# Attention, routed experts and a rational FFN in one launch: the last group's token ids placed ahead of its gates

## Chip, cores and metric

One core of a Trainium2 chip runs the whole program. The metric is the device time of one launch in microseconds (us); of several launches the median counts.

## What is computed

The reference chains three layers in fp32. Weights and activations are random normals.

```python
def _attn_ref(q, k, v):                      # 2 batches, 8 heads, 768 steps, 64 wide
    for t in range(S):
        state = gamma * state + outer(k[t], v[t])
        y[t] = scale * (q[t] @ state)

def _moe_ref(x, w_gate, w1, w2, capacity):   # 1536 tokens, 512 wide, 8 experts, 384 slots
    expert_idx = argmax(x @ w_gate); gate_w = softmax(...)[expert_idx]
    # token i takes the next slot of its expert, in the order of the tokens
    y = relu(disp @ w1) @ w2
    out[i] = gate_w[i] * y[expert_idx[i], pos[i]]

def _moe2_ref(x, w_in, w_out, a, b):
    h = x @ w_in
    g = (a0 + a1*h + a2*h**2 + a3*h**3) / (1 + |b0|*|h| + |b1|*h**2 + 1e-6)
    return g @ w_out
```

## The kernel before, in words

The order of the work on each engine is written out by hand (a manual schedule): every engine, and every DMA queue, does its own instructions strictly in the order of the code.

**Attention** (`attention`, L571) walks 12 units of 128 tokens; units 0 to 5 are one batch and 6 to 11 the other. For unit u TensorE does `scores` (L286: products of k and q into PSUM), `inter` (L314: the running state against q), `intra` (L332: masked scores against v) and `state` (L300). VectorE masks the scores (`mask`, L294) and scales the result (`attn_xt`, L343); ScalarE copies the state out (L312). `gate_mm` (L352) turns the unit's tokens round and forms the gate logits; `gate_out` (L411) copies the tokens out and SP writes them to the DRAM tensor `xd` (L420). Scores of unit u+1 are formed ahead of `inter(u)` if u is over 1 and behind `state(u)` if u is 0 or 1 (L631, L647). They all use one pair of PSUM banks, tag "s"; `inter` uses the pair "y" from unit 1 on.

**Routing.** The tokens are routed in two groups, units 0 to 6 and 7 to 11. Of a group, `gate_parts` (L383) finds expert and gate, `rank_mm` (L422) counts positions on TensorE, `rank_pos` (L458) turns them into slots, `rank_put` (L482) builds `pe` (a 0/1 matrix of rows) and `rr` (32 columns with the token ids and 32 with the gates, each in the column of its expert's tile), and `place_mm` (L495) multiplies them in full fp32, so that `tab` holds token id and gate of every slot. `rank_mm` of the second group also computes `self.pad` (L435 to L439), how far expert 0's first tile fell short of 128 tokens.

The first group's table gives 128 tokens of expert 0, fetched early (`early_gather`, L680) and put through that expert's first layer in `attn_tail` (L697). There the order on TensorE is: transposes of the fetched tokens (`early_x`), `gate_mm` of unit 11, ten first-layer matmuls (`win_l1`, L731; 12 for each half of the hidden units), `rank_mm`, two more, twelve more, `win_turn` of the first half (four transposes, L750), `place_mm` of the second group (L721), `win_turn` of the second half. VectorE meanwhile splits weights into a high and a low part (`split_lo`, L145; the low part alone is its work) and forms the low part of the turned activations (`win_parts`, L758). `indices` (L520) turns the ids of `tab` into `gidx`.

**Experts.** Then GpSimd (the POOL queue) gathers tiles 1, 2, 3 and on from `xd` (`gather`, L858; `fetch`, L848), which needs `gidx` and all writes to `xd`. `first_expert` (L807) does 14 of expert 0's 24 second-layer matmuls (`win_l2`, L765), turns gathered tile 1 (`expert_x`, L891: four transposes, a copy on ScalarE, a subtraction on VectorE), does the other ten and goes on with tile 1's 96 rows. Experts 1 to 7 and the FFN follow.

**Weight loads.** `load_next` (L160) issues on SP's queue; a load needs one of six `raw` buffers, and a buffer comes free when `split_lo` has read it. `attn_tail` asks for four (L707).

Of the kernel before, what the change touches and what calls it, by code (L numbers as in the profile page):

```python
# [7 lines left out]
F32 = mybir.dt.float32  # L8
# [13 lines left out]
E = 8  # L22
# [58 lines left out]
class Build:  # L81
# [70 lines left out]
    def load_w(self, i, half):  # L152
        nc = self.nc
        raw = self.wp.tile([128, 1024], F32, tag="raw", name="raw", bufs=6)
        sl = slice(half * 1024, half * 1024 + 1024)
        src = self.a["wm"][i] if i < 32 else self.wd[i - 32]
        nc.sync.dma_start(out=raw, in_=src[:, sl])
        self.raw[i, half] = raw

    def load_next(self, n):  # L160
        for _ in range(min(n, self.load_cap - self.nload)):
            self.load_w(self.nload // 2, self.nload % 2)
            self.nload += 1

    def prep_next(self):
# [119 lines left out]

    def scores(self, u):  # L286
        kt, qt = self.feats(u)
        sc = self.sc[u] = self.pair_bank("s", "sc").rearrange("p (r j t) -> p r j t", r=2, j=4)
# [133 lines left out]
    def rank_mm(self, b):  # L422
        nc = self.nc
        u0, u1 = self.units(b)
        g = u1 - u0
        oh = self.oh[:, u0:u1]
        bank = self.bank("rk")
        rk = bank[:, 0 : g * E].rearrange("p (g e) -> p g e", e=E)
        mms = [(rk, self.tri, oh[:, :, 0:E])]
        mms += [(rk[:, d:], self.ones, oh[:, 0 : g - d, 0:E]) for d in range(1, g)]  # L430
        if b:
            mms += [(rk[:, i], self.ones, self.run[:, 0:E]) for i in range(g)]
        for i, (out, w, x) in enumerate(mms):
            nc.tensor.matmul(out, lhsT=w, rhs=x, start=(i == 0), stop=(i == len(mms) - 1))
        if u0 == UA:  # L435
            cnt = bank[:, 64:65]
            nc.tensor.matmul(cnt, lhsT=self.ones, rhs=self.run[:, 0:1], start=True, stop=True)
            nc.vector.tensor_scalar(out=self.pad, in0=cnt, scalar1=-1.0, scalar2=128.0, op0=ALU.mult, op1=ALU.add)
            nc.vector.tensor_scalar(out=self.pad, in0=self.pad, scalar1=0.0, scalar2=None, op0=ALU.max)  # L439
        if u1 == NU:  # L440
            self.cnt = bank[:, 128 : 128 + 2 * E]
            for i in range(g + 1):
                x = oh[:, i - 1] if i else self.run
                nc.tensor.matmul(self.cnt, lhsT=self.ones, rhs=x, start=(i == 0), stop=(i == g))
        else:
# [36 lines left out]
    def rank_put(self, b):  # L482
# [2 lines left out]
        g = u1 - u0  # L485
        n = E * (self.nsub + 1)
        c2, pm, idk, gk = self.where.pop(b)
        at, rr, pe = sm("at", [g, n], bufs=1), sm("rr", [g, 2 * n]), sm("pe", [g, 128])
        tt(out=at, in0=self.over(self.col("slot"), g), in1=self.across(c2, g, n), op=ALU.is_equal)
        tt(out=rr[:, :, 0:n], in0=at, in1=self.across(idk, g, n), op=ALU.mult)  # L490
        tt(out=rr[:, :, n:], in0=at, in1=self.across(gk, g, n), op=ALU.mult)
        tt(out=pe, in0=self.over(self.col("iota"), g), in1=self.across(pm, g, 128), op=ALU.is_equal)
        self.place[b] = (pe, rr)

    def place_mm(self, b, tp=None):  # L495
        nc = self.nc
        pe, rr = self.place.pop(b)
        u0, u1 = self.units(b)
        n = E * (self.nsub + 1)
        tp = (self.bank("tpa", "tp") if tp is None else tp)[:, 0 : 2 * n]  # L500
        for i in range(u1 - u0):
            nc.tensor.matmul(tp, lhsT=pe[:, i], rhs=rr[:, i], start=(i == 0), stop=(i == u1 - u0 - 1))
        tp = tp.rearrange("p (a n) -> p a n", a=2)
        if b == 0:
            nc.vector.tensor_copy(self.tab, tp)
        else:
            nc.vector.tensor_tensor(out=self.tab, in0=self.tab, in1=tp, op=ALU.add)

    def count(self):
        self.nc.vector.tensor_copy(self.off, self.cnt)  # L510
# [60 lines left out]
    def attention(self):  # L571
        nc, tc, a = self.nc, self.tc, self.a
        with ExitStack() as st:
# [45 lines left out]
            for u in range(NU):  # L619
# [8 lines left out]
                    self.y_table(u + 3, pool)  # L628
                for n in LO_AT.get(u, ()):
                    self.split_lo(n // 2, n % 2)  # L630
                if 1 < u < NU - 1:  # L631
                    self.scores(u + 1)
                    self.mask(u + 1)
                if u - 2 in done:
                    next(gate)
                self.inter(u)
                if u - 4 in done:
                    self.place_mm(done[u - 4])
                if u == UA + 3:
                    self.early_gather()  # L640
                self.intra(u)
                if u:
                    self.attn_xt(u)
                if u - 2 in done:
                    next(gate)
                self.state(u)
                if u < 2:  # L647
                    self.scores(u + 1)
                    self.mask(u + 1)
                if u == 0:  # L650
# [22 lines left out]
                    self.rank_pos(done[u - 2])  # L673
                if u - 3 in done and not last:
                    self.rank_put(done[u - 3])
                for n in LO_END.get(u, ()):
                    self.split_lo(n // 2, n % 2)
            self.attn_tail()
# [18 lines left out]
    def attn_tail(self):  # L697
# [6 lines left out]
        self.gate_group(b)  # L704
        self.gate_out(u)
        ps.append(self.pair_bank("y", "l1")[:, 0:512])
        self.load_next(4)  # L707
        self.rank_mm(b)
        self.rank_pos(b)
        self.h0 = self.wp.tile([128, 2, 512], F32, tag="wt", name="h0", bufs=3)  # L710
# [3 lines left out]
        self.split_hi(3, 1)  # L714
        self.rank_put(b)
        self.count()
        self.split_lo(2, 1)
        self.win_l1(self.x0, ps, range(12, 24))
        self.win_relu(ps, self.h0, 1)
        t0 = self.win_turn(self.h0, 0, self.bank("tpa", "htp"))  # L720
        self.place_mm(b, self.pair_bank("s", "tp"))  # L721
        t1 = self.win_turn(self.h0, 1, self.bank("st", "htp"))
        self.indices(self.gidx, E * (self.nsub + 1))
        self.split_lo(3, 0)
        self.ht0 = self.win_parts(t0)
        self.split_lo(3, 1)
        self.ht1 = self.win_parts(t1)
        self.overfull()
        self.nprep = 8

    def win_l1(self, x, ps, seq):  # L731
# [73 lines left out]
        )  # L805

    def first_expert(self):  # L807
        bank = self.bank
        acc, hts = bank("l2"), (self.ht0, self.ht1)
        seq = [(0, i) for i in (0, 3, 6, 9, 1, 4, 7, 10, 2, 5, 8, 11)]  # L810
        seq += [(1, i) for i in (0, 3, 6, 9, 1, 4, 2, 5, 8, 11, 7, 10)]
# [528 lines left out]
```

## Time and profile before

| | |
|---|---|
| median of 3 runs | 519.93 us (519.87 to 520.26) |
| the profiled execution's own time | 519.19 us |
| its span, first to last instruction | 517.4 us |
| mean granted TensorE clock | 0.99 |
| TensorE / VectorE / ScalarE / GpSimd busy | 97% / 78% / 70% / 47% |

All times inside a trace count from the start of the span. A busy share is an average over stages. A timeline row gives start, duration, engine, line, operation, tiles written and read, and in brackets how long the engine stood idle before it and what released it. TensorE's matmuls overlap, so the distance between starts is what one costs, not its duration. PEclk is TensorE's granted clock: 1.00 is 2.4 GHz and 0.50 is 1.2 GHz.

### The profile page before, as it was taken

The page shows a single profiled execution, that of the slowest core. Times are in us where ns is not written, and L with a number is a line of the kernel's source. Part 1 is how long each engine was busy: PE and PEld are TensorE (multiplying, and loading weights), DVE is VectorE, ACT ScalarE, POOL GpSimd, SP SyncE. Part 2 cuts the span into 40 slices and gives each one's busy share as a digit, 9 for nine tenths or more (in the row PEclk, how much of TensorE's full clock was granted, in tenths as well). Part 3 has the DMA queues.
Part 4 walks back from the last instruction along what each step waited for, and adds up shares of the span by engine and source line. Part 5 has one row for each costly group of instructions (what it writes and reads, how often), then busy time and mean ns, then how long its engine had stood idle before and what let it go on. Part 6 is the DMA issues. An engine that isn't in the chain of part 4 may idle for free.

```text
span 517.4 us, 9416 instructions
## 1 busy us (share of the span) xinstructions
PE 504.2 (97%) x3538; PEld 442.2 (85%) x3538; DVE 403.4 (78%) x578; ACT 362.0 (70%) x588; POOL 244.1 (47%) x187
## 2 busy tenths in 40 slices
PE   7999979999999999999999999999999999999995
PEld 5888857999999999999988888888888888888884
DVE  3468753897887979786596989999899998865973
ACT  1345515877685867755697989999899987776760
POOL 2531040023331548153454546776667865445775
PEclk9999989999999999999999999999999999999998
DMA  8999761989977999994310002222022200000203
GB/s 318 405 415 366 216 224 39 300 292 306 323 267 272 366 284 302 295 277 165 104 60 1 0 2 82 82 81 82 1 81 86 79 1 0 1 0 0 83 21 143
DMA packets 27554, 83.08 MB, mean 161 GB/s; under 512 B 4976, under 2 KB 5360, under 8 KB 27504
## 3 DMA queue, kind: packets, MB, share of 16 engines
q1 hardware_dynamic: 24880, 75.09, 43.0%
q0 software_dynamic: 2624, 7.35, 4.0%
q8 instruction: 28, 0.46, 0.4%
q14 instruction: 22, 0.18, 0.1%
HBM read 71.93 MB, written 10.49 MB: 159 GB/s over the span
## 4 chain that ended last, share of the span: by engine, by line
PE 64%; DVE 1%; POOL 1%; issue 1%; ACT 1%; POOLq 0%; DVEq 0%
PE h L1046 8%; PE h L1048 8%; PE h L1047 8%; PE o L1119 7%; PE o L1118 7%; PE o L1117 7%; PE l L928 3%; PE l L930 3%; PE l L957 3%; PE l L929 3%; PE l L956 3%; PE l L955 3%; POOL out L1148 1%; PE tp L899 1%; DVE fw L1083 0%
## 5 line engine op out<-in xcount | busy, mean ns | idle before, releaser
L148 DVE TENSOR_TENSOR wlo<-raw,whi 128x1024 fp32r<-128x1024 f32 x80 | 109.8, 1387 | 14.3 <-ACT whi L143 14.0
L1097 POOL TENSOR_TENSOR gg<-fx,gg 128x512 fp32r<-128x512 f32 x47 | 61.2, 1302 | 70.0 <-issue 62.2
L143 ACT ACTIVATE whi<-raw 128x1024 fp32r<-128x1024 f32 x80 | 83.2, 1055 | 3.5 <-PE l L956 3.4
L1046 PE MATMUL h<-yh,whi 128*128 128x512 f32 x192 | 74.9, 390 | 0.0
L1117 PE MATMUL o<-whi,gg 128*128 128x512 f32 x192 | 74.8, 390 | 0.0
L1047 PE MATMUL h<-yl,whi 128*128 128x512 f32 x192 | 74.7, 389 | 0.0
L1048 PE MATMUL h<-yh,wlo 128*128 128x512 f32 x192 | 74.7, 389 | 0.0
L1118 PE MATMUL o<-wlo,gg 128*128 128x512 f32 x192 | 74.7, 389 | 0.0
L1119 PE MATMUL o<-whi,gg 128*128 128x512 f32 x192 | 74.7, 389 | 0.0
L1072 POOL TENSOR_TENSOR fw<-fh,fw 128x512 f32<-128x512 f32 x48 | 64.4, 1341 | 14.6 <-ACT fw L1061 13.8
L204 POOL TENSOR_TENSOR gq<-gq 128x512 int32<-128x512 int32 x16 | 26.7, 1666 | 86.7 <-DVE gq L201 60.9
L1059 ACT ACTIVATE fx<-h,ct 128x512 f32<-128x512 f32 x48 | 37.3, 777 | 38.2 <-PE h L1048 38.1
L928 PE MATMUL l<-xh,whi 128*128 128x224 f32 x224 | 62.0, 277 | 0.1
L955 PE MATMUL l<-hh,whi 128*128 128x224 f32 x224 | 61.9, 276 | 0.0
L930 PE MATMUL l<-xh,wlo 128*128 128x224 f32 x224 | 61.5, 275 | 0.0
L957 PE MATMUL l<-hh,wlo 128*128 128x224 f32 x224 | 61.5, 274 | 0.0
L956 PE MATMUL l<-hl,whi 128*128 128x224 f32 x224 | 61.4, 274 | 0.0
L929 PE MATMUL l<-xl,whi 128*128 128x224 f32 x224 | 61.4, 274 | 0.0
L928 PEld LDWEIGHTS l<-xh,whi 128*128 128x128 f32 x224 | 43.0, 192 | 0.4 <-ACT yh L794 0.3
L956 PEld LDWEIGHTS l<-hl,whi 128*128 128x128 f32 x224 | 43.0, 192 | 0.1
L955 PEld LDWEIGHTS l<-hh,whi 128*128 128x128 f32 x224 | 43.0, 192 | 0.1
L929 PEld LDWEIGHTS l<-xl,whi 128*128 128x128 f32 x224 | 43.0, 192 | 0.0
(161 smaller groups left out, 1176.7 us busy)
## 6 DMA issues: line engine op xcount, KB each, us to landing
raw<-wm SPq DMA_DIRECT2D x64, 512.0 KB, 6.6
r<-wf SPq DMA_DIRECT2D x32, 512.0 KB, 5.0
kv<-kv SPq DMA_DIRECT2D x22, 512.0 KB, 7.3
wd<-gq SPq DMA_DIRECT2D x16, 256.0 KB, 6.2
raw<-wd SPq DMA_DIRECT2D x8, 512.0 KB, 7.0
xd<-xs SPq DMA_DIRECT2D x12, 256.0 KB, 5.5
kv<-kv SPq DMA_DIRECT2D x4, 256.0 KB, 5.0
ca<-ct SPq DMA_DIRECT2D x1, 268.0 KB, 6.0
```

Source lines behind the costliest of these rows:

```text
L143: nc.scalar.activation(out=self.whi[i][:, sl], in_=raw, func=AF.Copy)
L148: (eng or self.nc.vector).tensor_tensor(out=self.wlo[i][:, sl], in0=raw, in1=self.whi[i][:, sl].bitcast(F32), op=ALU.subtract)
L928: nc.tensor.matmul(ps[:, fi], lhsT=wh[:, sl], rhs=xh[:, k], start=(k == 0), stop=False)
L929: nc.tensor.matmul(ps[:, fi], lhsT=wh[:, sl], rhs=xl[:, k], start=False, stop=False)
L955: mm(lhsT=wh[:, ws], rhs=fh, start=(f == 0 and o % 2 == 0), stop=False)
L956: mm(lhsT=wh[:, ws], rhs=fo, start=False, stop=False)
L1046: nc.tensor.matmul(h, lhsT=wh[:, sl], rhs=self.yh[:, k, ts], start=(k == 0), stop=False)
L1047: nc.tensor.matmul(h, lhsT=wh[:, sl], rhs=self.yl[:, k, ts], start=False, stop=False)
L1048: nc.tensor.matmul(h, lhsT=wl[:, sl], rhs=self.yh[:, k, ts], start=False, stop=(k == 3))
L1117: self.nc.tensor.matmul(ps, lhsT=gh[:, ms], rhs=wh[:, ws], start=first, stop=False)
L1118: self.nc.tensor.matmul(ps, lhsT=gh[:, ms], rhs=wl[:, ws], start=False, stop=False)
L1119: self.nc.tensor.matmul(ps, lhsT=gl[:, ms], rhs=wh[:, ws], start=False, stop=last)
```

## The change

`rr` gets three parts of 32 columns (ids, high part of the gate, low part of the gate). `rr` and `pe` become fp32r, so a placing matmul is one pass. A new `gate_put` builds the two gate parts, and `place_mm` takes a range of columns. The first group is placed in one go (`place_first`), which now also counts `pad`. In `attn_tail` the second group's ids are placed and turned into `gidx` before the last four first-layer matmuls, and its gates after four second-layer matmuls. The transposes of the first half go ahead of the ids. 20 of the 24 second-layer matmuls stand before `expert_x(0, 1)`. One weight load stays in the tail on SP; three are issued on ScalarE's queue behind `expert_x(0, 1)`. `overfull` moves behind them. In attention, scores of unit 1 move ahead of unit 0's `intra` (into bank pair "y"), and scores of unit 3 move behind `state(2)`.

```diff
@@ load_w, load_next
+    def load_w(self, i, half, eng=None):
-        nc.sync.dma_start(out=raw, in_=src[:, sl])
+        (eng or self.nc.sync).dma_start(out=raw, in_=src[:, sl])
@@ scores
-        sc = self.sc[u] = self.pair_bank("s", "sc")...
+        sc = self.sc[u] = self.pair_bank("y" if u == 1 else "s", "sc")...
@@ rank_mm
-        if u0 == UA:
-            cnt = bank[:, 64:65]
-            nc.tensor.matmul(cnt, lhsT=self.ones, rhs=self.run[:, 0:1], start=True, stop=True)
-            nc.vector.tensor_scalar(out=self.pad, in0=cnt, scalar1=-1.0, scalar2=128.0, op0=ALU.mult, op1=ALU.add)
-            nc.vector.tensor_scalar(out=self.pad, in0=self.pad, scalar1=0.0, scalar2=None, op0=ALU.max)
@@ rank_put
-        at, rr, pe = sm("at", [g, n], bufs=1), sm("rr", [g, 2 * n]), sm("pe", [g, 128])
+        at, rr, pe = sm("at", [g, n], bufs=1), sm("rr", [g, 3 * n], F32R, 1), sm("pe", [g, 128], F32R, 1)
...
-        tt(out=rr[:, :, n:], in0=at, in1=self.across(gk, g, n), op=ALU.mult)
...
+    def gate_put(self, b):
...
+        nc.vector.tensor_copy(gh, gk)
+        tt(out=gl, in0=gk, in1=gh.bitcast(F32), op=ALU.subtract)
+        for i, x in enumerate((gh.bitcast(F32), gl)):
+            tt(out=rr[:, :, n * (i + 1) : n * (i + 2)], in0=at, in1=self.across(x, g, n), op=ALU.mult)
+    def place_mm(self, b, tp, cols):
...
+        for i in range(g):
+            self.nc.tensor.matmul(tp[:, cols], lhsT=pe[:, i], rhs=rr[:, i, cols], start=(i == 0), stop=(i == g - 1))
+    def place_first(self):
+        nc, n = self.nc, E * (self.nsub + 1)
+        tp = self.bank("tpa", "tp")
+        self.place_mm(0, tp, slice(0, 3 * n))
+        cnt = tp[:, 128:129]
+        nc.tensor.matmul(cnt, lhsT=self.ones, rhs=self.run[:, 0:1], start=True, stop=True)
+        nc.vector.tensor_copy(self.tab[:, 0], tp[:, 0:n])
+        self.early_gather()
+        nc.vector.tensor_copy(self.tab[:, 1], tp[:, n : 2 * n])
+        self.place_add(1, tp[:, 2 * n : 3 * n])
...
@@ attention
-                if 1 < u < NU - 1:
+                if u == 0 or 2 < u < NU - 1:
                     self.scores(u + 1)
...
-                if u < 2:
+                if 0 < u < 3:
                     self.scores(u + 1)
...
                 if u - 3 in done and not last:
                     self.rank_put(done[u - 3])
+                    self.gate_put(done[u - 3])
@@ attn_tail
-        self.load_next(4)
+        self.load_next(1)
...
         self.rank_put(b)
         self.count()
+        self.win_l1(self.x0, ps, range(12, 20))
+        t0 = self.win_turn(self.h0, 0, self.bank("xk", "htp"))
+        n = E * (self.nsub + 1)
+        tp = self.pair_bank("s", "tp")
+        self.place_mm(b, tp, slice(0, n))
+        self.place_add(0, tp[:, 0:n])
+        self.indices(self.gidx, n)
+        self.win_l1(self.x0, ps, range(20, 24))
+        ht0 = self.win_parts(t0)
+        self.win_relu(ps, self.h0, 1)
+        self.acc0, self.hts = self.bank("l2"), [ht0]
+        self.win_l2(self.hts, self.acc0, [(0, i) for i in (0, 3, 6, 9)], last=False)
+        self.gate_put(b)
+        t1 = self.win_turn(self.h0, 1, self.bank("st", "htp"))
         self.split_lo(2, 1)
-        self.win_l1(self.x0, ps, range(12, 24))
-        self.win_relu(ps, self.h0, 1)
-        t0 = self.win_turn(self.h0, 0, self.bank("tpa", "htp"))
-        self.place_mm(b, self.pair_bank("s", "tp"))
-        t1 = self.win_turn(self.h0, 1, self.bank("st", "htp"))
-        self.indices(self.gidx, E * (self.nsub + 1))
+        tp = self.pair_bank("y", "tp")
+        self.place_mm(b, tp, slice(n, 3 * n))
+        self.hts.append(self.win_parts(t1))
         self.split_lo(3, 0)
-        self.ht0 = self.win_parts(t0)
+        for i in (1, 2):
+            self.place_add(1, tp[:, i * n : i * n + n])
         self.split_lo(3, 1)
-        self.ht1 = self.win_parts(t1)
-        self.overfull()
@@ first_expert
-        self.win_l2(hts, acc, seq[:14], last=False)
+        seq = [(0, i) for i in (2, 5, 8, 11, 1, 4)] + [(1, i) for i in (0, 3, 6, 9)]
+        seq += [(0, i) for i in (7, 10)] + [(1, i) for i in (2, 5, 8, 11)]
+        self.win_l2(hts, acc, seq, first=False, last=False)
         self.expert_x(0, 1)
+        self.load_next(3, nc.scalar)
+        self.overfull()
         self.rows()
-        self.win_l2(hts, acc, seq[14:], first=False)
+        self.win_l2(hts, acc, [(1, i) for i in (1, 4, 7, 10)], first=False)
```

## Rows read from the trace of the kernel before

**Rows 1.** The page, part 1: busy time, share of the span, instructions.
```profile
PE 504.2 (97%) x3538; PEld 442.2 (85%) x3538; DVE 403.4 (78%) x578; ACT 362.0 (70%) x588; POOL 244.1 (47%) x187
```

**Rows 2.** Windows: length, busy time of PE, PEld, DVE, ACT, POOL; PEclk, DMA share, GB/s.
```profile
73.20:73.40 0.20, 0.00 (x0) 0.00 (x0) 0.00 (x0) 0.00 (x0) 0.08 (x1) 0.88 0.96 389
...
80.00:81.00 1.00, 1.00 (x5) 0.65 (x5) 0.00 (x0) 0.55 (x1) 0.00 (x0) 0.91 0.00 0
...
100.00:110.00 10.00, 10.00 (x93) 10.00 (x92) 7.64 (x11) 9.42 (x15) 0.03 (x1) 1.00 0.90 360
```

**Rows 3.** Timeline of PE around the second gather.
```profile
66.27 1.23 PE L502 MATMUL tp<-rr,pe 128*128 128x64 f32 x10
...
67.69 1.17 PE L771 MATMUL l<-whi,ht 128*128 128x512 f32 x4
...
75.05 1.09 PE L899 MATMUL tp<-ct,xg 128*128 128x128 f32 x4 [3.64 <-DMA xg<-xd,gidx]
...
80.20 0.39 PE L736 MATMUL l<-whi,xh 128*96 128x512 f32 x1
```

**Rows 4.** Timelines of DVE and POOL: from the table to the second gather.
```profile
67.53 0.22 DVE L507 TENSOR_TENSOR tab<-tab,tp 128x64 f32<-128x64 f32 x1 [0.74 <-PE tp L502]
...
68.25 1.73 POOL L849 DMA_INDIRECT xg<-xd,gidx  x1 [13.86 <-DVE gidx L522]
```

**Rows 5.** DMA from issue to landing: second gather, early gather, last write of xd; SP's issues.
```profile
xg<-xd,gidx POOLq DMA_INDIRECT x1, 6.7
...
DMA to landing us min/median/max: 3.7/3.7/3.7
...
xd<-xs SPq DMA_DIRECT2D x1, 256.0 KB, 4.6
...
61.36 0.33 SPq L420 DMA_DIRECT2D xd<-xs  x1
...
70.89 0.33 SPq L157 DMA_DIRECT2D raw<-wm  x1
```

**Rows 6.** Timelines of PE and DVE: the second group's ranks and matrices.
```profile
62.14 0.17 PE L444 MATMUL rk<-run,ones 128*128 128x16 bf16 x1 [0.25 <-DVE pad L438]
...
64.70 1.10 PE L736 MATMUL l<-whi,xl 128*128 128x512 f32 x4
...
62.48 0.20 DVE L468 TENSOR_TENSOR hit<-rk,oh 128x40 f32<-128x40 f32 x1 [0.20 <-PE rk L444]
...
64.75 0.82 DVE L492 TENSOR_TENSOR pe<-ct,pm 128x640 f32<-128x640 f32 x1
```

**Rows 7.** Start-up: landing of unit 1's k and q, its issue, PE, ACT.
```profile
kv<-kv SPq DMA_DIRECT2D x1, 512.0 KB, 5.2
...
2.61 0.43 SPq L242 DMA_DIRECT2D kv<-kv  x1
...
7.38 1.09 PE L341 MATMUL yt<-scm,kv 128*64 128x128 f32 x16 [0.91 <-DVE kv L268]
...
11.41 1.09 PE L341 MATMUL yt<-scm,kv 128*64 128x128 f32 x16 [0.78 <-POOL qd L263]
...
8.99 0.39 ACT L312 ACTIVATE s<-st 128x256 f32<-128x256 f32 x1 [6.95 <-PE st L341]
```

**Rows 8.** Timelines of DVE, PE and POOL: the first group's placing and the early gather.
```profile
48.93 0.38 DVE L491 TENSOR_TENSOR rr<-at,gk 128x224 f32<-128x224 f32 x1
...
50.58 1.66 PE L502 MATMUL tp<-rr,pe 128*128 128x64 f32 x13
...
53.19 1.21 POOL L849 DMA_INDIRECT xg<-xd,gidx  x1 [7.31 <-DMA xd<-xs]
...
57.55 0.60 PE L689 MATMUL xtp<-ct,xg 128*128 128x128 f32 x4
```

**Rows 9.** Timeline of ACT behind the second gather.
```profile
83.16 0.59 ACT L745 ACTIVATE h<-l 96x512 f32<-96x512 f32 x1 [2.02 <-PE l L736]
...
91.06 2.00 ACT L143 ACTIVATE whi<-raw 128x1024 fp32r<-128x1024 f32 x2
```

More of the change, by code (lines that the diff above doesn't have):

```diff
@@ L150, in split_lo @@
         )
-    def load_w(self, i, half):
-        nc = self.nc
+    def load_w(self, i, half, eng=None):
         raw = self.wp.tile([128, 1024], F32, tag="raw", name="raw", bufs=6)
@@ L156, in load_w, with load_next @@
         src = self.a["wm"][i] if i < 32 else self.wd[i - 32]
-        nc.sync.dma_start(out=raw, in_=src[:, sl])
+        (eng or self.nc.sync).dma_start(out=raw, in_=src[:, sl])
         self.raw[i, half] = raw
-    def load_next(self, n):
+    def load_next(self, n, eng=None):
         for _ in range(min(n, self.load_cap - self.nload)):
-            self.load_w(self.nload // 2, self.nload % 2)
+            self.load_w(self.nload // 2, self.nload % 2, eng)
             self.nload += 1
@@ L287, in scores @@
         kt, qt = self.feats(u)
-        sc = self.sc[u] = self.pair_bank("s", "sc").rearrange("p (r j t) -> p r j t", r=2, j=4)
+        sc = self.sc[u] = self.pair_bank("y" if u == 1 else "s", "sc").rearrange("p (r j t) -> p r j t", r=2, j=4)
         for j in range(4):
@@ L487, in rank_put @@
         c2, pm, idk, gk = self.where.pop(b)
-        at, rr, pe = sm("at", [g, n], bufs=1), sm("rr", [g, 2 * n]), sm("pe", [g, 128])
+        at, rr, pe = sm("at", [g, n], bufs=1), sm("rr", [g, 3 * n], F32R, 1), sm("pe", [g, 128], F32R, 1)
         tt(out=at, in0=self.over(self.col("slot"), g), in1=self.across(c2, g, n), op=ALU.is_equal)
         tt(out=rr[:, :, 0:n], in0=at, in1=self.across(idk, g, n), op=ALU.mult)
-        tt(out=rr[:, :, n:], in0=at, in1=self.across(gk, g, n), op=ALU.mult)
         tt(out=pe, in0=self.over(self.col("iota"), g), in1=self.across(pm, g, 128), op=ALU.is_equal)
-        self.place[b] = (pe, rr)
@@ L495, in place_mm @@
[L495 to L507, printed above, removed]
+        self.place[b] = (pe, rr, at, gk)
@@ new lines, in gate_put @@
+    def gate_put(self, b):
+        nc, sm, tt = self.nc, self.small, self.nc.vector.tensor_tensor
+        _, rr, at, gk = self.place[b]
+        _, g, n = at.shape
+        gh, gl = sm("gh", [g], F32R), sm("gl", [g])
+        nc.vector.tensor_copy(gh, gk)
[3 more added lines that the diff above has]
+    def place_mm(self, b, tp, cols):
+        pe, rr, _, _ = self.place[b]
+        g = pe.shape[1]
+        for i in range(g):
+            self.nc.tensor.matmul(tp[:, cols], lhsT=pe[:, i], rhs=rr[:, i, cols], start=(i == 0), stop=(i == g - 1))
@@ new lines, in place_first @@
+    def place_first(self):
[8 more added lines that the diff above has]
+        self.place_add(1, tp[:, 2 * n : 3 * n])
+        nc.vector.tensor_scalar(out=self.pad, in0=cnt, scalar1=-1.0, scalar2=128.0, op0=ALU.mult, op1=ALU.add)
+        nc.vector.tensor_scalar(out=self.pad, in0=self.pad, scalar1=0.0, scalar2=None, op0=ALU.max)
@@ L509, in count, with place_add @@
+    def place_add(self, i, tp):
+        self.nc.vector.tensor_tensor(out=self.tab[:, i], in0=self.tab[:, i], in1=tp, op=ALU.add)
     def count(self):
@@ L637, in attention @@
                 if u - 4 in done:
-                    self.place_mm(done[u - 4])
-                if u == UA + 3:
-                    self.early_gather()
+                    self.place_first()
                 self.intra(u)
@@ L807, in first_expert @@
     def first_expert(self):
[L808 to L811, printed above, removed]
-        self.win_l2(hts, acc, seq[:14], last=False)
+        nc, bank = self.nc, self.bank
+        acc, hts = self.acc0, self.hts
+        seq = [(0, i) for i in (2, 5, 8, 11, 1, 4)] + [(1, i) for i in (0, 3, 6, 9)]
+        seq += [(0, i) for i in (7, 10)] + [(1, i) for i in (2, 5, 8, 11)]
+        self.win_l2(hts, acc, seq, first=False, last=False)
         self.expert_x(0, 1)
+        self.load_next(3, nc.scalar)
+        self.overfull()
         self.rows()
-        self.win_l2(hts, acc, seq[14:], first=False)
+        self.win_l2(hts, acc, [(1, i) for i in (1, 4, 7, 10)], first=False)
         y = self.y_rows(acc, 0)
```

## The prediction, made before the changed kernel was built or run

> **What bounds the kernel now.** I read the page first: TensorE is busy for 97% of the span [rows 1], so time can only come from the few places where it stands still or runs slowly, or from work taken off it. The windows say which. In the experts' stage it is busy without a break at a granted clock of 1.00, though the DMA engines are at 0.90 [rows 2]: whatever shifts the start of that stage shifts its end, as long as weights keep arriving. The timeline of TensorE shows one big stop, 3.64 us up to 75.05, waiting for gathered tile 1, so its last matmul before that ended at 71.41 [rows 3]. In the windows the clock falls from 2.4 to 1.2 GHz inside that stop (0.88 between 73.20 and 73.40) and comes back only at the start of 80 to 81 (0.91) [rows 2]. So four transposes and ten second-layer matmuls, from 75.05 to 80.20 [rows 3], ran at half clock too. The chain of the stop is: table addition at 67.53, gather issued at 68.25 [rows 4], landed 6.7 us later [rows 5], which is 74.95.
>
> **The second group's ids (tail).** Four things set when this gather can go.
>
> Ranks: today the second group's `rank_mm` counts the padding too, and TensorE waits 0.25 us for VectorE to read that count; the count matmul itself is about 0.15, like the one beside it [rows 6]. Both leave, so the ranks, and `hit` on VectorE, come 0.4 earlier. TensorE gains this 0.4 as well.
>
> Matrices: the gate product leaves the chain. It takes 0.38 for 224 columns [rows 8], so about 0.25 for 160. `pe` then starts at 64.75 - 0.4 - 0.25 = 64.10 and ends at 64.92 [rows 6].
>
> TensorE's side: the last four first-layer matmuls start at 64.70 and take 1.10 [rows 6], the transposes follow until 66.27 [rows 3], that is 0.47. In the new order the transposes come before those four, so they end at 64.70 - 0.4 + 0.47 = 64.77, and the ids' pass waits about 0.2 for `pe`. That is a new wait on TensorE, with first-layer matmuls queued behind it: **+0.2**.
>
> Passes: placing takes ten instructions and 1.23 us now [rows 3], two per matmul. An fp32r matmul costs 0.108 from start to start (93 in 10.00 us [rows 2]); five for ids and five for gates make 1.08. I count **0**: a part saved is spent on the second pass. The Trainium skill (FP8 and Floating Point Precision, TensorE Precision Notes) gives true fp32 four passes where reduced fp32 has one; by it the two parts would take a half of 1.23, and the result would be some 0.6 lower, 513.3. The trace speaks against so much, since its fp32r matmuls don't go below 0.108.
>
> So the ids are in PSUM at 64.97 + 0.54, some 65.55 with 0.04 for the hand-over; addition, `gidx` and issue take 0.72 more, as from 67.53 to 68.25 today [rows 4]: about 66.35, some 1.9 us earlier. The gather also needs the last write to `xd`, issued at 61.36 and landed 4.6 later, at 65.96 [rows 5]; this no longer has much to spare but doesn't decide.
>
> **When tile 1 is there, and when it is wanted.** The early gather, with hardly any weight traffic beside it, landed after 3.7 us; the second took 6.7 with weight loads issued around it up to 70.89 [rows 5]. The change leaves one of four loads in the tail, so I take the 3.7 end: landed at 70.1, at the latest 73.1. TensorE comes to its transposes at 71.41 - 0.4 + 0.2 plus six more second-layer matmuls; 14 took 71.41 - 67.69 = 3.72 [rows 3], so 0.25 each without their small wait, 1.5 together: 72.7. The tile is there. At the bad end TensorE would wait 0.4, too little to matter.
>
> **Gap and clock.** The stop goes: **-3.64**. With no long stop the clock stays, and 5.15 us of work shrinks. Halving all of it gives back 2.6; pricing it by rows at full clock, 0.47 for the transposes and ten at 0.25, gives 2.2. I take **-2.4**, the middle.
>
> VectorE gets more small operations (`gate_put`, a second addition) and its splits come later. Its last weight split of the tail freed the buffer for the load at 70.89 [rows 5] and now ends near 72.0; its reader, the second half of the last four matmuls, runs at 73.5. Hidden, and without that cover it would cost the difference, under 1 us.
>
> **The three loads and ScalarE.** They are issued behind the copy of tile 1, near 73.5. No row shows a DMA issued by ScalarE. SP's take 0.33 each [rows 5], about 1.3 us with pauses; below that, nothing. Behind them wait the output copy and the ReLU that stood at 83.16 [rows 9] and will be wanted at 77.2, so 2.4 us is spare: cost 0. Their buffers are free by then. Loads landed at 80 serve splits that stood at 91.06 and later [rows 9], now 85: cost 0. SP's queue only loses work.
>
> **The first group.** Its 14 fp32 instructions (13 took 1.66 [rows 8]) become seven of 0.108 and the count: TensorE gains 0.8 of work, of which 0.4 goes in waiting, since VectorE's one gate product of 0.38 [rows 8] becomes two with two small operations, 0.65 more. VectorE is the late one there, behind it come a mask and the table copy, so the early gather leaves at 53.85 instead of 53.19 and lands 3.7 later at 57.55, exactly when TensorE wanted it [rows 8]. **0**; bounds -0.4 (the gather in time) and +0.7 (all of the delay).
>
> **Start-up.** Unit 1's k and q land at 2.61 + 5.2 = 7.81 [rows 7]. `scores(1)`, 1.1 us long, now goes first, so unit 0's `intra` moves from 7.38 to about 8.95: +1.57. Behind `state(0)` the scores are gone (-1.1), but they had covered the copy of the state, 0.39 [rows 7] and its hand-overs: +0.5. The 0.78 stop at 11.41 [rows 7] goes, as the mask of unit 1 is ready. Sum **+0.2**. The later stop at a mask only moves on by one unit. Bounds: -0.2 (k and q land 0.4 sooner) and +0.6.
>
> **Sum.** +0.2 + 0 - 0.4 + 0.2 - 3.64 - 2.4 = -6.0. The profiled execution took 519.19, so 513.2; the median of the runs is 0.74 above it, so **513.9** for the median. A measurement of this kernel tells a difference of some 0.2% (1 us) from none.
>
> **Rivals.**
> 1. *The clock falls elsewhere* (0.08). TensorE now idles from 6.47 to 7.85 in the start-up, longer than its 0.91 there [rows 7] and shorter than the idle time before the fall at 73.3. The half-clock stretch of today cost 2.4, so 516.3; at most 3.4, half of the 6.8 us at 0.50. The Trainium skill (TensorE: Matmul & The Clock Gate, Part 1) says that idleness halves the clock and work restores it; the trace agrees at 73.3 and 80.2, but no row shows a stop of this size.
> 2. *The early gather decides* (0.10): its 0.65 delay stays on the path, and start-up takes its upper bound. 513.9 + 0.7 + 0.4 = 515.0.
> 3. *The change doesn't do what it says* (0.05): the gather is still not there, held by the last write to `xd` or by descriptor work on GpSimd, 1.73 beside a split [rows 4]. The point is a landing 2 us behind TensorE's 72.7, since then clock and gap both return: 513.9 + 2 + 2.4 = 518.3, up to 520. Only a landing 8.4 us after the issue does that, and the slowest of these rows is 6.7.
> 4. *Weights arrive late* (0.02): the experts' stage has DMA at 0.90 [rows 2], and a stage with so little to spare could eat the gain: about 519.9. Against it: its loads are paced by buffers, which come 6 us earlier too.
> 5. *Slower: ScalarE is stuck in its DMA issues* (0.03). It works in order. The 2.4 to spare plus 1.3 are used up when one issue takes over 1.2; to lose the 6 gained as well, with 2.4 of it through the clock falling in the new stop, an issue must cost (3.7 + 3.6) / 3 = 2.4. At 3 us each: 513.9 + 9.0 - 3.7 + 2.4 = 521.6. SP's 0.33 speaks against it, and no row shows ScalarE's own.
>
> **How the numbers follow.** The forecast has 0.72, with a range of its own from 513.0 (both lower bounds, and the clock's 2.6) to 514.8. To hold 8 in 10 the range takes in rival 2 and the nearer end of rival 1: **512.9 to 516.3**. Faster by over 0.2%: forecast, rivals 1 and 2 and most of 3, 0.93; same: the rest of 3 and rival 4, 0.03; slower 0.04.
>
> **What would show it.** Right: no stop over 0.5 us ahead of tile 1's four transposes, PEclk 1.00 from 60 to 100, the gather issued near 66.5 and landed in under 4.5, tile 1's first layer starting near 74.2 instead of 80.20, `intra` of unit 0 near 8.95. Wrong: a stop there with 0.50 behind it; a second clock fall in the first 20 us; long stops of TensorE on ScalarE's ReLU behind the three issues; or new stops on weight splits after 85, which would give the gain back.

## The result, and the profile after

The changed kernel took 513.49 us in the median of four runs (513.12 to 513.91), the kernel before 519.90 beside it (518.17 to 520.26): a ratio of 0.989, with a 95% interval of 0.986 to 0.992. The prediction was 513.9, range 512.9 to 516.3. The profiled executions took 519.19 before and 513.91 after, spans 517.4 and 512.1; 5.3 us lie between these two, 6.4 between the medians.

The page of the changed kernel, its parts 1 and 3. TensorE's share rises from 97% to 98% [rows 1]; q10 is new, the queue on which ScalarE issued three weight transfers.

```profile
PE 500.3 (98%) x3531; PEld 439.3 (86%) x3531; DVE 405.4 (79%) x588; ACT 361.9 (71%) x588; POOL 243.9 (48%) x187
...
q10 hardware_dynamic: 432, 1.57, 0.9%
```

Windows of the changed kernel: length, busy time of PE, PEld, DVE, ACT and POOL, then PEclk, DMA share and GB/s. Before, the clock fell inside the stop ahead of tile 1 and was back only at 80 to 81 [rows 2]. Here it is 1.00 in all four, and between 58 and 75 TensorE stands still for 0.09 us in all.

```profile
58.00:75.00 17.00, 16.91 (x107) 13.96 (x108) 13.53 (x41) 7.22 (x17) 4.73 (x4) 1.00 0.56 175
...
74.00:80.00 6.00, 6.00 (x32) 4.38 (x31) 2.56 (x15) 2.75 (x5) 2.22 (x3) 1.00 0.88 259
75.00:95.00 20.00, 20.00 (x134) 16.60 (x133) 14.95 (x30) 14.97 (x22) 3.60 (x4) 1.00 0.84 263
100.00:110.00 10.00, 10.00 (x92) 10.00 (x91) 8.92 (x11) 7.02 (x10) 2.04 (x1) 1.00 0.80 282
```

Timeline of PE of the changed kernel (start, length, line, out<-in; a bracket is the idle time before it and what ended it). These answer to [rows 3], [rows 6] and [rows 8]. Four marks divide the kernel: the early tile's transposes (`xtp`), the ids' pass (five matmuls 32 wide), tile 1's four transposes (`tp<-ct,xg`) and tile 1's first layer (the first matmul of 96).

```profile
52.39 0.98 PE L502 MATMUL tp<-rr,pe 128*128 128x96 f32 x7 [1.16 <-DVE rr L496]
...
58.86 0.64 PE L699 MATMUL xtp<-ct,xg 128*128 128x128 f32 x4
...
66.29 0.73 PE L502 MATMUL tp<-rr,pe 128*128 128x32 f32 x5
66.87 1.17 PE L756 MATMUL l<-whi,xl 128*128 128x512 f32 x4
...
69.17 0.72 PE L502 MATMUL tp<-rr,pe 128*128 128x64 f32 x5
69.73 1.17 PE L791 MATMUL l<-whi,ht 128*128 128x512 f32 x4
...
73.47 0.60 PE L921 MATMUL tp<-ct,xg 128*128 128x128 f32 x4
73.83 1.18 PE L791 MATMUL l<-wlo,ht 128*128 128x512 f32 x4
74.85 0.41 PE L756 MATMUL l<-whi,xh 128*96 128x512 f32 x1
```

Tile 1's transposes have no bracket: the stop of 3.64 us is gone. Tile 1's first layer stands at 74.85 instead of 80.20, 5.35 earlier, and from there to the end of the span it is 437.2 us in both kernels (517.4 - 80.20 and 512.1 - 74.85). So the whole difference is made before tile 1, and the experts' stage gives nothing back. The way there splits in two: `xtp` comes 1.31 later (57.55 to 58.86), and from `xtp` to tile 1's first layer it takes 15.99 instead of 22.65, **6.66 less**.

### The profile page after: what moved, and what is told of

Same layout as the page of the kernel before. It is cut to its first block, busy times and chain, and to the rows that moved or that the text cites. A ratio compares the mean times of both kernels' runs of the same rounds, so it can differ in the third digit from the quotient of the medians.

```text
span 512.1 us, 9408 instructions
## 1 busy us (share of the span) xinstructions
PE 500.3 (98%) x3531; PEld 439.3 (86%) x3531; DVE 405.4 (79%) x588; ACT 361.9 (71%) x588; POOL 243.9 (48%) x187
## 4 chain that ended last, share of the span: by engine, by line
PE 65%; DVE 1%; POOL 1%; issue 1%; ACT 1%; POOLq 0%; DVEq 0%
PE h L1068 9%; PE h L1069 9%; PE h L1070 8%; PE o L1140 7%; PE o L1139 7%; PE o L1141 7%; PE l L950 3%; PE l L952 3%; PE l L979 3%; PE l L978 3%; PE l L951 3%; PE l L977 3%; POOL out L1170 1%; PE tp L921 1%; DVE fw L1105 0%
```

## The experiments

Twelve kernels ran, each beside the kernel before: the first four on one chip, the next four and the last four on two others. The kernel before had medians of 518.27, 518.22 and 518.49 there (51 runs, 515.66 to 520.38), lower and wider than in the comparison above. The last column is the time from `xtp` to tile 1's first layer, which leaves out what differs between executions in the start-up; it is 22.65 in the profile before and 15.99 in the one after. The ratio is the comparison's own estimate, not the quotient of the two medians.

| kernel | median us (range, runs) | ratio to before, 95% | gather issued, us after xtp | xtp to tile 1 |
|---|---|---|---|---|
| changed (e8) | 513.22 (512.50–513.59, 6) | 0.990 [0.988, 0.993] | 9.42 | 15.83 |
| e1 four loads on SP | 513.29 (512.86–515.01, 6) | 0.989 [0.986, 0.992] | 8.88 | 15.98 |
| e2 old start-up | 513.46 (512.88–515.24, 6) | 0.990 [0.987, 0.993] | 8.82 | 15.93 |
| e3 ids four matmuls later | 513.81 (513.46–515.99, 6) | 0.991 [0.988, 0.994] | 9.45 | 16.25 |
| e4 before + cover + late loads | 513.04 (512.67–514.08, 6) | 0.989 [0.986, 0.991] | 10.68 | 16.43 |
| e5 before + cover | 515.61 (514.75–517.95, 12) | 0.996 [0.994, 0.998] | 10.70 | 18.39 |
| e6 before + late loads | 514.21 (513.96–515.27, 6) | 0.993 [0.990, 0.996] | 10.69 | 17.52 |
| e7 early ids, no cover, loads on SP | 513.51 (512.81–517.60, 12) | 0.993 [0.990, 0.995] | 8.85 | 15.97 |
| e9 before + 12 more matmuls | 517.37 (516.18–518.86, 12) | 0.998 [0.996, 0.999] | 10.70 | 19.91 |
| e10 seven more warm-ups | 513.86 (513.55–514.43, 6) | 0.991 [0.988, 0.994] | 8.79 | 15.91 |
| b1 e4 + padding early | 513.51 (512.88–514.21, 6) | 0.990 [0.988, 0.993] | 10.28 | 16.03 |
| b2 gates of group one later | 513.02 (512.48–513.39, 5) | 0.989 [0.986, 0.992] | 8.87 | 15.98 |

In all twelve, tile 1's first layer to the end of the span takes 437.1 to 437.3 us, but for e2, whose profiled execution had one later stop (below).

The changed kernel itself ran again beside three of them, as the measure for the others:

> The changed kernel as it is, for comparison on the same chip: 513.0 to 513.9, with single executions up to 515.5 where the granted clock falls behind the stop of 2.2 us in the start-up.

The expectation held: it took 513.22, 0.3 below the first comparison, and its profile has no stop at tile 1 either (transposes at 72.87, first layer at 74.24).

**Three remedies for one stop.** The change does three things about the second gather: ids earlier, three loads out of its way, six more second-layer matmuls as cover (20 ahead of the transposes, not 14). Which of them is needed?

e4 puts the last two alone into the kernel before, e5 the cover alone, e6 the loads alone:

```diff
# e5 (e4 has this and e6's)
-        self.win_l2(hts, acc, seq[:14], last=False)
+        self.win_l2(hts, acc, seq[:20], last=False)
         self.expert_x(0, 1)
# e6
-        self.load_next(4)
+        self.load_next(1)
...
         self.expert_x(0, 1)
+        self.load_next(3, self.nc.scalar)
```

> The kernel before with two edits alone: 20 in place of 14 second-layer matmuls ahead of the transposes of tile 1, and three of the tail's four weight loads issued on ScalarE behind it. Ids and gates stay together in fp32, the padding stays in the second group, the start-up is the old one. Theory (these two edits hold the gain; the rest costs about as much in attention as it brings): gather issued at 68.3, landed at 72.1, TensorE there at 72.9, no stop, PEclk 1.00: 512.5 to 513.8. Rival (early ids and the padding bring 2 us or more): 515 to 517, with a stop of 1 us or more ahead of the transposes.

> The kernel before with one edit: 20 in place of 14 second-layer matmuls ahead of the transposes of tile 1. Theory (the slow landing, 6.7 us beside three weight loads, is what makes the stop): gather issued at 68.3 to 69.3, landed near 75.5, TensorE there 1.4 later than before, a stop of 2 to 2.5 us is left, and in the executions where the granted clock falls in it 2 us more are lost; 514.5 to 517.0. Rival (six matmuls of cover are enough by themselves): 513.0 to 513.8, stop under 0.5.

> The kernel before with one edit: three of the four weight loads of the tail issued on ScalarE behind tile 1's copy; 14 matmuls ahead, as before. Theory (landing time decides): the gather lands 3.8 us after its issue, a stop of 0.5 to 1.0 us is left, PEclk stays 1.00, and the kernel takes 513.2 to 514.2. Rival (cover of six matmuls needed as well): stop of 2 us or more and a clock that falls, 516 or more.

Timeline of PE of e5, at tile 1's transposes and first layer:

```profile
74.86 0.63 PE L899 MATMUL tp<-ct,xg 128*128 128x128 f32 x4 [1.74 <-DMA xg<-xd,gidx]
...
76.25 0.42 PE L736 MATMUL l<-whi,xh 128*96 128x512 f32 x1
```

The same of e6:

```profile
72.42 0.63 PE L899 MATMUL tp<-ct,xg 128*128 128x128 f32 x4 [0.89 <-DMA xg<-xd,gidx]
...
75.19 0.39 PE L735 MATMUL l<-whi,xh 128*96 128x512 f32 x1
```

The timelines of POOL and PE of e4, and its second gather from issue to landing:

```profile
69.32 1.73 POOL L849 DMA_INDIRECT xg<-xd,gidx  x1 [13.63 <-DVE gidx L521]
...
73.71 0.60 PE L899 MATMUL tp<-ct,xg 128*128 128x128 f32 x4
...
xg<-xd,gidx POOLq DMA_INDIRECT x1, 3.9
```

All three theories held, though e6's median is 0.01 above its range. Cover alone leaves a stop of 1.74, late loads alone one of 0.89, both together none. In these executions neither remaining stop lowers the clock: four transposes and ten matmuls take 75.19 - 72.42 = 2.77 in e6, 5.15 before. (Two runs of e5 took 517.17 and 517.95 at 0.994 and 0.993; they have no profile.) In e4 the gather is issued as long after `xtp` as in the kernel before (10.68, 10.70) but lands after 3.9 instead of 6.7. So the loads beside it were what made it slow, and e4, without any of the early ids, reaches the changed kernel's time.

The other side: e7 keeps the early ids, with no cover and four loads on SP; e1 keeps ids and cover and puts the loads back on SP.

```diff
# e1, and e7 too
-        self.load_next(1)
+        self.load_next(4)
...
-        self.load_next(3, nc.scalar)
# e7 alone: 14 matmuls ahead of the transposes, as before
-        self.win_l2(hts, acc, seq, first=False, last=False)
+        self.win_l2(hts, acc, seq[:10], first=False, last=False)
```

> The changed kernel with all four weight loads issued in the tail on SP, as before, and none on ScalarE. Theory (the gather lands in 3.8 us only because the loads are out of its way): it lands some 6.5 us after its issue near 69.4, so at 75.9; TensorE, there at 73.5, stops 2 to 2.5 us, and if the granted clock falls in that stop some 2 more are lost. 515.5 to 518 against 513.5. Rival (the gather's speed does not hang on the loads, and the order of the matmuls alone did it): no stop over 0.5 us, 513.0 to 514.0.

> The changed kernel with the other two remedies taken back: four loads in the tail on SP, and 14 matmuls ahead of the transposes. Early ids, the padding and the new start-up stay. Theory (the change also moves VectorE's weight splits behind the ids, so the loads that wait for their buffers leave after the gather by themselves): gather lands in 3 to 4 us, stop of 0 to 0.7, 513.3 to 514.3. Rival (early ids alone bring 1 to 2 us of the gather's time and no more): a stop of 1.5 us or more, 515 to 517.

The timelines of POOL, PE and SP (DMA issues) of e7, and last, of the kernel before, that of SP:

```profile
67.50 1.00 POOL L870 DMA_INDIRECT xg<-xd,gidx  x1 [11.37 <-DVE gidx L533]
...
71.87 0.60 PE L920 MATMUL tp<-ct,xg 128*128 128x128 f32 x4
...
69.73 3.76 SPq L156 DMA_DIRECT2D raw<-wm  x3
...
66.82 4.41 SPq L157 DMA_DIRECT2D raw<-wm  x3
```

The early ids alone are enough too in this execution, as e7's theory had it, and e1's theory of a stop missed: the gather leaves 1.85 us earlier against `xtp` than in the kernel before, and tile 1 is there when TensorE comes. SP's three loads leave 2.2 us behind the gather although the program gives them to SP early. Before, the first of them left 1.43 us ahead of it (66.82 against 68.25). They wait for buffers that VectorE's splits free, and in the new order those splits stand behind the ids. Moving the ids therefore moves the loads as well, and handing them to ScalarE adds nothing that shows (e1: 513.29, the changed kernel 513.22 on another chip).

Whether the early ids do without the cover in every execution isn't shown. Two of e7's twelve runs took 517.05 and 517.60, more than any run of a kernel that has the cover as well (515.99 at most), and its ratio of 0.993 comes from means, 514.23 against 513.12 for e8. A gather held as in the first profile of the changed kernel, issued 10.50 after `xtp` and landed 3.8 later, would come at 14.3, where e7's TensorE asked at 13.22: a stop of some 1.1. No slow run of e7 has a profile, so this is an estimate from rows of other kernels.

Against the 518.22 of that chip late loads alone are worth 4.0, the cover alone 2.6, the early ids alone 4.7, together 11.3; all three give 5.0. They cure one and the same stop: in the profiles the early ids, with the loads that they move, close it by themselves (e7 also has the padding and the new start-up), and the other two do so together.

e3 moves the ids' pass behind all twelve first-layer matmuls of the second half.

```diff
-        self.win_l1(self.x0, ps, range(12, 20))
+        self.win_l1(self.x0, ps, range(12, 24))
...
-        self.win_l1(self.x0, ps, range(20, 24))
```

> The changed kernel with the ids' pass put back behind all twelve first-layer matmuls of the second half, so the ids come some 1 us later; all else stays. Theory (the second gather is held by the landing of the last write of xd at 68.5, not by the ids): the gather goes at 69.4 to 69.9 all the same, TensorE stops 0 to 0.5 us, 513.4 to 514.1. Rival (the ids set the gather, as the prediction has it): gather 1 us later, at 70.4, landing at 74.2, a stop of 0.7 to 1.0, 514.2 to 514.6. That placing the ids early is the main source of the gain would show as more than 515.

The gather left 9.45 after `xtp`, 0.6 later than in e1, and tile 1 had no stop; 513.81 lies in the theory's range, though not by its reason: the gather followed `gidx` by 0.46 (67.71, 68.17), so here the ids set it and not the write, as in the rival, but without the rival's stop. The place of the ids in the order isn't tight.

**The clock.** e9 keeps the kernel before and lets TensorE run twelve matmuls more in the stop, into a bank that nobody reads.

```diff
         self.win_l2(hts, acc, seq[:14], last=False)
+        self.win_l2(hts, bank("l1"), [(0, 0)] * 12)
         self.expert_x(0, 1)
```

> The kernel before with 12 more second-layer matmuls ahead of the transposes, into a bank that nobody reads: 2.8 us of work that the result does not need, in the place of the stop. Theory (the stop costs its own length, and 2 to 2.5 us more where the granted clock falls in it): the clock stays at 1.00, and the kernel takes 516.2 to 517.2 in all executions, against a median of 518.2 that spreads from 515.7 to 520.4. Rival (the spread of the kernel before comes from elsewhere): the same spread, median 518 or above, since work was added.

Timeline of PE of e9, a window of e9, and last the same stretch of the kernel before:

```profile
76.01 0.66 PE L900 MATMUL tp<-ct,xg 128*128 128x128 f32 x4 [0.53 <-DMA xg<-xd,gidx]
...
78.79 0.39 PE L736 MATMUL l<-whi,xh 128*96 128x512 f32 x1
...
76.00:79.00 3.00, 2.99 (x15) 2.51 (x16) 1.51 (x8) 0.49 (x1) 0.99 (x1) 1.00 0.84 292
...
75.05:80.20 5.15, 5.15 (x15) 4.15 (x15) 2.14 (x11) 0.49 (x1) 1.00 (x1) 0.50 0.50 181
```

The gather is issued as late as before, and the work is the same from the transposes to tile 1: 2.78 us instead of 5.15. That is **2.37 for the clock**, at 1.2 GHz before and at 2.4 here. The median falls by only 1.1, because the clock does not fall in every execution of the kernel before. Its 51 runs show it: fourteen took 519.59 or more, at mean granted clocks of 0.989 to 0.993, sixteen took 517.58 or less, at 0.996 to 0.999, and the rest lie between. In e9 none takes over 518.86, at clocks of 0.996 to 0.999. The forecast of 516.2 to 517.2 for all was too narrow, as seven of twelve lie above it. The clock accounts for the upper end of the spread; what spreads the rest isn't shown.

**The start-up.** e2 gives the changed kernel the old order there; e10 keeps the new one and runs ten warm-up matmuls instead of three ahead of `scores(1)`.

```diff
# e2
-        sc = self.sc[u] = self.pair_bank("y" if u == 1 else "s", "sc").rearrange("p (r j t) -> p r j t", r=2, j=4)
+        sc = self.sc[u] = self.pair_bank("s", "sc").rearrange("p (r j t) -> p r j t", r=2, j=4)
...
-                if u == 0 or 2 < u < NU - 1:
+                if 1 < u < NU - 1:
...
-                if 0 < u < 3:
+                if u < 2:
# e10
-WA, WC = 7, 3
+WA, WC = 7, 10
```

> The changed kernel with the scores of units 1 and 3 where they stood before. Theory (the new start-up waits for unit 1's k and q with nothing to do, and delays all): attention from unit 3 on runs 0.5 to 0.6 us earlier, and the kernel takes 512.9 to 513.1 against 513.5. Rival (the end of attention is set by VectorE and the early gather, so a start-up gain is swallowed there): 513.3 to 513.7. Rival from the prediction (0.2 us): 513.3.

> The changed kernel with ten in place of three warm-up matmuls behind the first scores, which fill some 1.9 us of the stop of 2.2 us in the start-up. Theory (the new start-up risks a fall of the granted clock in that stop, seen in one profile at 0.50 around 10 us): the median stays at 513.2, and no execution lies above 514.5 with a clock of 0.995 or less. Rival (the high executions have another cause): the same tail. If the filling delays the scores, 0.2 to 0.4 more.

In the medians the new start-up is worth nothing either way (513.46, against 513.29 for e1 on the same chip and 513.22 for e8 on another, ranges overlapping): e2's theory missed and its rival held. Its risk shows in the profiled execution of e1, which has it unchanged. A timeline row of PE and two windows of e1:

```profile
8.60 1.65 PE L340 MATMUL sc<-kv 64*128 64x128 f32 x12 [2.08 <-DMA kv<-kv]
...
9.00:11.00 2.00, 2.00 (x20) 1.78 (x20) 0.28 (x1) 0.00 (x0) 1.32 (x2) 0.50 1.04 409
11.00:13.00 2.00, 1.74 (x32) 1.60 (x28) 1.70 (x3) 0.21 (x1) 1.75 (x2) 0.79 1.02 405
```

Behind a stop of 2.08 us for unit 1's k and q TensorE ran at 0.50, that is 1.2 GHz, and this execution took 515.01, 1.7 above the median of e1. The profiles of the changed kernel and of e3 have stops of 2.22 and 2.73 in the same place, and the clock stays at 1.00. So the stop can lower the clock and mostly doesn't. Five more runs with this start-up took 515.15 or more (e3 one, e7 four, at 0.993 to 0.995); they have no profile, and in e7 the missing cover may be the cause. But e2, with the old order, has a run of 515.24 at 0.995 as well, so such runs aren't all due to the new order. In e10 the stop is gone (warm-ups until 8.42, `scores(1)` at 8.36) and no run is over 514.43. That doesn't prove the point, as no run of e8 is over 513.59 without the filling. Its median is 0.6 higher than e8's, on another chip; `scores(4)`, at 20.37 against 20.05 in e8, gives half of that, the rest is open.

e2's profiled execution also shows a stop of 1.0 behind ScalarE's `x_gate` (L911) that no other has; where it comes from stays open.

**Looking for something faster.** b1 adds to e4 the padding counted at the first group. b2 is the changed kernel with the old start-up, and places only the first group's ids in unit 10, its gates one unit later.

```diff
# b1, beside e4's edits
+            self.pcnt = bank[:, 128:129]
+            nc.tensor.matmul(self.pcnt, lhsT=self.ones, rhs=self.run[:, 0:1], start=True, stop=True)
...
                     self.early_gather()
+                    self.pad_put()
# b2, in place_first
-        self.place_mm(0, tp, slice(0, 3 * n))
+        self.place_mm(0, tp, slice(0, n))
```

> The kernel before with 20 matmuls ahead, three loads on ScalarE, and the padding counted at the first group; ids and gates stay together in fp32, no early ids, old start-up. Theory (the padding is worth its 0.4 us, and without the gate operations on VectorE attention ends earlier): 512.4 to 512.9, 0.3 to 0.8 under the changed kernel. Rival (the differences below 1 us are swallowed by collisions of VectorE with GpSimd): 513.0 to 513.4.

> The changed kernel with the old start-up, and with the first group's gates built behind unit 10's masks and placed in unit 11, so that its ids and the early gather come first. Theory (VectorE is late there by the gate operations and TensorE waits for them and for the early gather): the transposes of the early gather start near 57.0 in place of 58.4 to 58.9, and the kernel takes 512.0 to 512.6. Rival (the gates' operations move to a place where VectorE is as late): 513.0 to 513.6.

b1's tail is shorter than e4's by exactly the 0.40 of the padding (16.03, 16.43), and its profiled execution took 513.44 against 514.08, yet its median is 0.5 higher instead of lower, and above both of its forecasts; between kernels on two chips so little can't be told. b2's early gather leaves at 53.94 and `xtp` starts at 58.39, not at the 57.0 hoped for: the gates' pass, moved to the next unit, now stands on TensorE shortly ahead of it (56.58 to 57.38) and waits 0.21 for VectorE there. Its rival held. Both lie within the noise of the changed kernel; no version that ran is clearly faster.

## Why the prediction was right, point by point

**The mechanism holds.** The stop of 3.64 is gone, the clock is 1.00, the later weights arrive in time, and 437.2 us behind tile 1 are untouched. Each half of the forecast has its own evidence: the clock's -2.4 is the 2.37 of e9, and the stop is closed in the profile of every kernel that has the early ids, or the cover with the late loads.

**The tail gained 6.66 where the sum had 6.24** (-0.4 + 0.2 - 3.64 - 2.4). Ranks: the stretch from the first rank matmul to the first-layer matmul behind it was 0.83 (61.47 to 62.30) and is 0.42 (62.78 to 63.20), -0.41 as forecast. The new wait for `pe`: 65.60 to 66.29 for transposes that took 0.47, so +0.22 as forecast. Passes: the two take 0.58 and 0.56 (66.29 to 66.87, 69.17 to 69.73), 1.14 from start to start against 1.06 before, so about nothing, as taken. The Trainium skill (FP8 and Floating Point Precision, TensorE Precision Notes) has four passes for true fp32, one for each product of the high and low parts; with one pass for the reduced form, these would have halved, and the trace does not agree at this width. The 0.108 behind my 0 was read from a stretch of matmuls mostly 224 columns wide; that 32 and 64 columns cost no less (0.116 and 0.112) was not in those rows, so the term came out right by luck. The mis-sized term is the second-layer matmuls: the fourteen that took 3.72 up to the stop I left as they were, but the sixteen behind 69.73 take 3.74, 0.234 each, so fourteen are worth 3.28. That is 0.44, small waits and the run-out of the pipe ahead of the stop, and it is the difference; the remaining terms, among them the passes' +0.08 and -0.09 in the first-layer matmuls around the ids' pass, cancel.

**Start-up and first group were 0 and +0.2 in the sum; the pair of profiles says +1.31.** Read step by step, as rows of the changed kernel's PE timeline:

```profile
8.26 1.16 PE L340 MATMUL sc<-kv 64*128 64x128 f32 x16 [2.22 <-DMA kv<-kv]
9.35 1.09 PE L340 MATMUL yt<-scm,kv 128*64 128x128 f32 x16
...
11.39 0.67 PE L340 MATMUL yt<-kv,s 64*64 64x128 f32 x16 [0.48 <-DVE xt L348]
...
20.27 1.16 PE L340 MATMUL sc<-kv 64*128 64x128 f32 x16 [0.20 <-DVE scm L297]
```

Unit 1's k and q landed after 5.6, not 5.2 [rows 7], and unit 0's `intra` started at 9.35, not 8.95; `scores(4)`, the row at 20.27, stood at 19.69 before: +0.58. From there to `xtp` it is 38.59 instead of 37.86: +0.73, my upper bound of 0.7, the first group's gates delaying the early gather. But one execution of each is a poor measure of tenths. Eight profiles with the old start-up (before, e2, e4, e5, e6, e9, b1, b2) have `scores(4)` at 19.59 to 20.25, median 20.0; of five with the new one (the changed kernel, e1, e3, e7, e8) three have it at 20.05 to 20.27, e3 at 20.98 behind a later landing of k and q, e1 at 22.11. So +0.2 is what it mostly costs, with a long tail above it. The stop for unit 1's k and q, which rival 1 put at 1.4 (6.47 to 7.85), was 1.39 to 2.73 in these five. For the first group, five profiles with the old one (before, e4, e5, e6, e9) have `xtp` 37.86 to 38.63 behind `scores(4)`, median 38.3; seven with the new one (the changed kernel, e1, e2, e3, e7, e8, e10) 37.74 to 38.59, median 38.4: some 0.1, nearer to my 0 than to the pair's 0.73.

What VectorE was doing there was not foreseen. Timelines of DVE and POOL of the changed kernel, in the gates of the first group:

```profile
42.24 0.98 DVE L398 TENSOR_TENSOR eq<-eq,ct 128x56 f32<-128x56 f32 x1
...
45.61 0.70 DVE L405 TENSOR_SCALAR su<-su 128x7 f32<-128x7 f32 x1
...
42.11 1.04 POOL L267 TENSOR_TENSOR kv<-kv,ca 128x512 f32<-128x512 f32 x1 [4.17 <-DMA kv<-kv]
45.24 1.04 POOL L267 TENSOR_TENSOR kv<-kv,ca 128x512 f32<-128x512 f32 x1 [2.09 <-PE xk L361]
```

The same two operations took 0.22 and 0.17 before. Each now ends about when a GpSimd operation that runs beside it does (at 43.15 and 46.28): 1.3 us on the engine that is late there, of which the kernel before already had 0.44 (its `jj`, L474, took 0.62 beside such an operation, 0.18 here). The rest, with 0.58 for the gates' own operations and 0.58 for the start-up, makes up the 2.02 by which the table copy comes later (52.50, 54.52). It differs between executions: in e8, the same kernel, the two took 0.22 and 0.35. The Trainium skill (SBUF — State Buffer, SBUF: two separate sides) tells of a port pair that a VectorE operation with two inputs in SBUF, or in a two-port mode, and a GpSimd operation that reads SBUF take in turns, each for its whole length. The first row agrees, 0.98 with its end where GpSimd's 1.04 end; the second has one input, and no row shows its mode.

**The second gather** left 1.6 us later than its ids allowed. Timelines of DVE and POOL of the changed kernel, and its DMAs from issue to landing (last write of `xd`; gather):

```profile
67.28 0.18 DVE L533 TENSOR_SCALAR gidx<-tab 128x32 int32<-128x32 f32 x1
...
69.36 1.46 POOL L871 DMA_INDIRECT xg<-xd,gidx  x1 [12.98 <-DVE rr L496]
...
xd<-xs SPq DMA_DIRECT2D x1, 256.0 KB, 5.8
...
xg<-xd,gidx POOLq DMA_INDIRECT x1, 3.8
```

Before, the gather followed `gidx` by 0.46 (67.79, 68.25), so here it could go at 67.74; the forecast 66.35 plus the 1.31 of the prelude is 67.66. The last write of `xd`, issued at 62.67, landed only at 68.5: 5.8 us instead of the 4.6 that I took [rows 5]. This is the start of rival 3 (the bracket's name for the releaser is inferred, and the gather doesn't read `rr`). That the write held it is read from the times; no run tests it. By this reading the step "doesn't decide" fell in this execution. Of the 0.9 us between that landing and GpSimd's start, some 0.5 are more than the hand-over from `gidx` took, and remain unexplained. It cost nothing: landed after 3.8, close to my 3.7, tile 1 was there at 73.2 for transposes at 73.47. In e1, e2, e7, e10 and b2 it followed `gidx` by 0.46, so the write did not hold it, and the gather left 8.79 to 8.88 after `xtp` instead of 10.70: 1.9 earlier, the forecast's figure. In e8 it followed by 1.14, and no row gives the write's landing there.

**ScalarE's issues** cost nothing, as forecast. Timeline of ACT of the changed kernel:

```profile
74.26 1.35 ACTq L156 DMA_DIRECT2D raw<-wm  x3
75.71 0.69 ACT L802 ACTIVATE y<-l,tab 128x512 f32<-128x512 f32 x1 [0.98 <-DVE ovf L526]
77.82 0.59 ACT L765 ACTIVATE h<-l 96x512 f32<-96x512 f32 x1 [1.42 <-PE l L756]
```

Three issues take 1.35, and the ReLU still waits 1.42 for TensorE, not TensorE for it: rival 5 needed 2.4 each. From 80 to 500 us TensorE has no stop on a weight (it is busy for 419.82 of these 420), so rival 4 is out.

**Rival 1** was a real mechanism: in e1 TensorE ran at 0.50 behind its stop in the start-up. The Trainium skill (TensorE: Matmul & The Clock Gate, Part 1) lets idleness halve the clock; e1's window agrees, in the start-up as the kernel before does in the tail, though by the runs here it needs not happen in each execution. Its 515.01 is below the 516.3 that I gave it.

**Where forecast and measurement met partly by luck.** The sum went against a profiled execution in which the clock fell. On the chip where it ran again (e8), and where the kernel before often kept its clock, the changed kernel gains 5.0 (513.22 against 518.22), not 6.4. The level of the changed kernel was right; the gain depends on which executions of the kernel before it is held against. Two errors also met: the sum gave 513.2 for the profiled execution, which took 513.91, 0.7 more (+1.11 in the prelude, -0.42 in the tail), and the 0.74 then added for the median did not return, as the median lies 0.42 below that execution. Small slips in the working changed nothing: 65.55 and 0.72 make 66.27, not 66.35, and the lower bounds with the clock's 2.6 add up to 512.9, not 513.0.

## What to carry to other kernels

When several edits go at one stop, don't add their worth: try each alone and in pairs, since the first that closes the stop takes all of it, and a simple pair (here a longer cover and three later loads) may do for the whole change. A stop of TensorE is priced twice, by its length and by the work behind it at the lower clock, and the second part shows only in some executions. Before an edit of tenths is read from one pair of profiles, set marks in the program and compare the stretches between them over several executions.

## What the runs showed of the hardware that was not expected

- The last write of `xd`, 256 KB, landed after 3.2 to 5.8 us in the profiles that give a time for it alone; in one of them a gather whose ids were ready 5.1 us behind that issue left later than its ids allowed.
- A gather of 128 rows took 3.2 to 3.9 us where no weight load was issued just ahead of it or in the 2 us behind its issue, and 6.7 where three were issued from 66.82 on, 1.43 ahead of it.
- VectorE operations of 0.2 us stretched to 0.6, 0.7 and 0.98 beside a GpSimd operation of 1.04.
- A DMA issue on ScalarE's queue took 0.38 us by itself, and three took 1.35 with their pauses; SP's took 0.33 to 0.43 [rows 5, rows 7].
- The clock's fall is not the same in every execution: in the same place a stop of 2.08 us had 0.50 behind it in one execution, and stops of 2.22 and 2.73 had 1.00 in two others.
